# A list-scheduled attention and MLP kernel: the sign step of the weight unpacking gets a place outside the softplus/erf stretches, and the dates of many other steps move

## The chip, the cores and the metric

The kernel runs on one core of a Trainium2 chip. The metric is device time in microseconds (us). The core's engines are TensorE (PE, with its weight loads as PEld), VectorE (DVE), ScalarE (ACT), GpSimd (POOL) and SyncE (SP, which here issues nearly all DMAs). Each engine works through its own instructions in the order in which the program lists them, and waits at each for what that instruction needs.

## The reference

A linear ("random feature") attention over 8 x 8 heads gives x, and a gated MLP follows it. Cut to what matters:

```
phi(x)  = exp(x @ omega.T - |x|^2/2 - max) / sqrt(128)     # 128 features, head width 64
attn    = (phi(q) @ (phi(k).T @ v)) / (phi(q) @ sum(phi(k)) + 1e-6)    # 8 x 8 heads, 576 tokens
x       = attn, laid out as 4608 tokens x 512
h       = x @ w_in                                         # 512 -> 2048
g       = h * erf(softplus(h))
out     = g @ w_out                                        # 2048 -> 512
```

## The kernel before

**Work and tiles.** The heads are taken in 32 pairs. For a pair, `project` makes the features (tiles `ppk`, `ppq`, then `fk`, `fq` by exponentials on ACT), `key_values` sums keys times values (`kvp`, copied to `kh`), `turn` transposes the query features (`pt`, copied to `qh`), and `attend` multiplies both (`nd`) and divides by way of a logarithm and an exponential on ACT (`rc`), which gives `xs`. The 4608 tokens form six groups, `SUPERS`: groups 0 and 1 with half-widths of 288 columns, groups 2 to 5 with 432. In groups 2 to 5 the projections are done with seven instead of eight block products (a scheme with sums of blocks: `hX`, `hY`, `hZ`, and `oX`, `oY`, `oZ` from group 3 on). Groups 0 and 1 use the plain products `h` (names h000 to h110) and `o`. Every product of fp32 numbers is made of three matmuls on a high and a low part (`xh`, `xl`; `gh`, `gl`; the two halves of a weight tile `w`).

**Softplus/erf stretches.** Each group is cut into four quarters of the 2048 hidden units, so there are 24 stretches (`chain`). A stretch is four ACT instructions on the `gs` tiles: softplus, softplus, erf, erf. The two functions are in two different activation tables, and the exponentials and logarithms of the attention are in a third; an `ACT_TABLE_LOAD` stands wherever the table has to change. Then DVE or POOL multiplies (`gate`: `hs<-gs,hs`), and `high`/`rest` split the result into `gh`/`gl`. In groups 3 to 5 (eleven stretches) the steps `gsum` first form differences of blocks in `gs`, and `th`, `tl`, `bh`, `bl`, `bb` are split from them. The tile names carry group and granule: the second stretch of group 0 works on gs0_2 and gs0_3, the third on gs0_4 and gs0_5.

**Weights.** The weights come in as 64-bit words. In group 0 and at the start of group 1, `make` unpacks each of 32 tiles: a DMA (`st`), then `pbias` on ACT, an `ACTIVATE` with the function Prelu that brings in sign and exponent (`wt<-st`), `ptail` (`st<-st`) and `pjoin` (`wt<-wt,st`) on DVE, `phigh` on ACT or DVE (the high half of `w`), `prest` on DVE (the low half), and a store. Only then can TensorE use the tile. Later uses fetch the finished tile back. w1_... are tiles of the first projection and w2_... of the second; w2_0_3_0 and w2_0_3_1 are the last tiles that the first and the second quarter's `o` use.

**What sets the order.** `Plan.order` writes every engine's instruction list before anything runs. Each step has a due time; a list of small shifts (`JITTER`) moves the due times of steps in a window; distances between engines (`LAG`), buffer numbers and the options (which engines a step may go to, at what cost, with how much slack) do the rest. A step may name the activation table it needs (`set`). While a softplus/erf stretch is under way, only steps without a `set` may be placed on ACT, and a change of table is charged `COST["table"]`. Where the plan itself returns to the exponential's table, it writes the load; other loads are added when the program is built, wherever an instruction's function isn't in the table that is loaded. In the kernel before, `pbias` names no table.

All engines' instructions go through one helper, so the line in the rows is the same everywhere (L1015 before, L1049 after); tiles tell them apart.

## Time and profile before

| | before |
|---|---|
| median of 3 runs | 1029.24 us (1028.66 to 1030.05) |
| the profiled execution, its own time | 1027.2 us |
| its span in the trace | 1025.4 us |
| mean granted TensorE clock (1.0 is 2.4 GHz) | 0.997 |
| PE busy | 1003.5 us (98%) |
| PEld / DVE / ACT / POOL busy | 932.8 / 795.0 / 688.5 / 612.9 us |
| activation table loads | 72, together 92.4 us |
| first matmul starts, last one ends | 3.74 us, 1021.13 us |

The span is the profiled execution between its first and last instruction; 1.8 us of the execution's own time lie outside it. Busy times are sums over the whole span, so the share says little on any one place. PE busy counts an instruction until its modelled end, so it doesn't tell fast matmuls from slow ones.

### The profile page before, as it was taken

The page shows a single profiled execution, that of the slowest core. Times are in us where ns is not written, and L with a number is a line of the kernel's source. Part 1 is how long each engine was busy: PE and PEld are TensorE (multiplying, and loading weights), DVE is VectorE, ACT ScalarE, POOL GpSimd, SP SyncE. Part 2 cuts the span into 40 slices and gives each one's busy share as a digit, 9 for nine tenths or more (in the row PEclk, how much of TensorE's full clock was granted, in tenths as well). Part 3 has the DMA queues.
Part 4 walks back from the last instruction along what each step waited for, and adds up shares of the span by engine and source line. Part 5 has one row for each costly group of instructions (what it writes and reads, how often), then busy time and mean ns, then how long its engine had stood idle before and what let it go on. Part 6 is the DMA issues. An engine that isn't in the chain of part 4 may idle for free.

```text
span 1025.4 us, 19428 instructions
## 1 busy us (share of the span) xinstructions
PE 1003.5 (98%) x7132; PEld 932.8 (91%) x7132; DVE 795.0 (78%) x1284; ACT 688.5 (67%) x1295; POOL 612.9 (60%) x446
## 2 busy tenths in 40 slices
PE   8999999999999999999999999999999999999998
PEld 7799889999999999999999888989989999989997
DVE  5788878877876976677787987798887687678664
ACT  8988776787685774765768585677657655644650
POOL 3625443875567816455788356489884668957520
PEclk9999999999999999999999999999999999999999
DMA  8377776699686766676657866656786457686751
GB/s 229 90 267 237 255 239 244 240 320 307 218 298 205 255 213 220 225 243 202 223 187 277 280 224 214 226 199 212 246 278 223 164 185 227 219 288 219 230 180 70
DMA packets 99486, 232.72 MB, mean 227 GB/s; under 512 B 11200, under 2 KB 11712, under 8 KB 99392
## 3 DMA queue, kind: packets, MB, share of 16 engines
q1 hardware_dynamic: 99232, 231.42, 67.5%
q8 instruction: 57, 0.93, 0.4%
q14 instruction: 37, 0.30, 0.1%
q10 hardware_dynamic: 160, 0.07, 0.0%
HBM read 188.45 MB, written 42.99 MB: 226 GB/s over the span
## 4 chain that ended last, share of the span: by engine, by line
PE 84%; DVE 6%; issue 3%; ACT 2%; DMA 2%; POOL 1%; SPq 1%; POOLq 0%; DVEq 0%; ACTq 0%
PE o L1015 17%; PE hX L1015 13%; PE h L1015 10%; PE oX L1015 9%; PE hY L1015 6%; PE nd L1015 5%; PE oY L1015 4%; PE ppq L1015 4%; PE ppk L1015 4%; PE kvp L1015 4%; PE hZ L1015 3%; PE pt L1015 2%; PE oZ L1015 2%; DMA uq<-qT 1%; DVE gs L1015 1%
## 5 line engine op out<-in xcount | busy, mean ns | idle before, releaser
L1015 PE MATMUL o<-gh,w 128*128 128x288 f32 (+1 forms) x832 | 213.5, 329 | 0.6 <-DVE w L1015 0.6
L1015 POOL TENSOR_TENSOR hs<-gs,hs 128x864 f32<-128x864 f32 (+1 forms) x50 | 112.2, 2266 | 106.1 <-ACT gs L1015 85.2
L1015 PE MATMUL hX<-xh,wb 128*128 128x432 f32 x512 | 168.6, 369 | 2.4 <-ACT hs L1015 1.4
L1015 PEld LDWEIGHTS o<-gh,w 128*128 128x128 f32 x832 | 145.2, 188 | 6.4 <-DVE w L1015 1.2
L1015 PE MATMUL o<-gl,w 128*128 128x288 f32 (+1 forms) x416 | 132.9, 319 | 0.1
L1015 PE MATMUL h<-xh,w 128*128 128x288 f32 x512 | 127.9, 318 | 5.0 <-DVE w L1015 4.4
L1015 PEld LDWEIGHTS hX<-xh,wb 128*128 128x128 f32 x512 | 96.2, 188 | 8.6 <-ACT hs L1015 1.8
L1015 POOL TENSOR_TENSOR uq<-uq 128x288 f32<-128x288 f32 (+1 forms) x50 | 50.9, 1038 | 79.2 <-DMA uq<-qN 38.9
L1015 PEld LDWEIGHTS h<-xh,w 128*128 128x128 f32 x512 | 89.0, 193 | 9.5 <-DVE w L1015 5.6
L1015 ACT ACT_TABLE_LOAD x72 | 92.4, 1283 | 2.0 <-PEq L1368 0.7
L1015 PE MATMUL hX<-xl,wb 128*128 128x432 f32 x256 | 91.6, 358 | 0.0
L1015 ACT ACTIVATE fk<-ppk,mxk 128x128 f32<-128x128 f32 x288 | 81.2, 379 | 8.9 <-DVE mxk L1015 8.0
L1015 PE MATMUL hY<-xh,wb 128*128 128x432 f32 x256 | 84.8, 368 | 0.0
L1015 ACT ACTIVATE fq<-ppq,mxq 128x128 f32<-128x128 f32 x288 | 78.1, 386 | 8.2 <-DVE mxq L1015 7.9
L1015 PE MATMUL oX<-th,wb 128*128 128x432 f32 x264 | 82.9, 361 | 0.0
L1015 PEld LDWEIGHTS o<-gl,w 128*128 128x128 f32 x416 | 78.3, 188 | 2.7 <-DVE gl L1015 0.5
L1015 ACT ACTIVATE rc<-nd,eps 64x288 f32<-64x288 f32 x128 | 63.4, 496 | 25.2 <-PE nd L1015 22.2
L1015 ACT ACTIVATE hs<-hX 128x432 f32<-128x432 f32 x71 | 37.1, 529 | 63.2 <-PE hX L1015 62.3
L1015 PE MATMUL nd<-qh,kh 128*128 128x288 f32 x256 | 76.3, 410 | 1.9 <-DVE qh L1015 1.4
L1015 PE MATMUL h<-xl,w 128*128 128x288 f32 x256 | 76.9, 300 | 0.7 <-POOL xl L1015 0.7
L1015 DVE TENSOR_TENSOR xs<-nd,rc 64x288 f32<-64x288 f32 (+1 forms) x160 | 61.2, 393 | 16.6 <-ACT rc L1015 11.1
L1015 ACT ACTIVATE gs<-hs 128x1728 f32<-128x1728 f32 (+1 forms) x48 | 69.4, 1481 | 1.1 <-POOL bl L1015 0.8
(141 smaller groups left out, 2642.4 us busy)
## 6 DMA issues: line engine op xcount, KB each, us to landing
wb<-wdc SPq DMA_DIRECT2D x216, 256.0 KB, 3.6
wb<-wdw SPq DMA_DIRECT2D x162, 256.0 KB, 3.9
w<-wdw SPq DMA_DIRECT2D x52, 512.0 KB, 4.7
st<-w SPq DMA_DIRECT2D x32, 512.0 KB, 4.9
wdw<-w SPq DMA_DIRECT2D x32, 512.0 KB, 4.3
wdc<-c SPq DMA_DIRECT2D x32, 512.0 KB, 4.7
v<-vP SPq DMA_DIRECT2D x32, 325.0 KB, 5.2
uk<-kR SPq DMA_DIRECT2D x24, 320.0 KB, 3.9
```

Of the source, the lines that this page charges most:

```text
L1015: return tc.keep_in_program_order(method(*args, **kwargs))
```

## The change

One step gets a table: `pbias` now says `set="exp"`, so the planner no longer places it inside a softplus/erf stretch. The list of shifts is replaced (15 entries before, five of them empty and the others with the position in the list as their seed; 131 entries now, each with its own seed), and nearly all constants of the planner move a little: the distances `LAG`, the offsets of due times (`DRAIN`, `DIVIDE`, `FIRST`), and the slacks with which a step goes to POOL (`GATES`, `RESTS`, `LATE`, `WHG`) or ACT (`SQA`). What is computed, and each instruction's form, stay; the numbers of some engines' instructions move since steps change engine.

```diff
-LAG = {"T": 0.32725, "A": 0.2525, "V": 0.2605, "G": 0.3105, "S": 0.2904}
+LAG = {"T": 0.33004999999999995, "A": 0.26025, "V": 0.261, "G": 0.3147, "S": 0.32880000000000004}
...
-        for k, (lo, hi, amp) in enumerate(JITTER):
+        for lo, hi, amp, k in JITTER:
...
+JITTER = ((227.5, 727.5, 4, 5), (648.5, 748.5, 1, 874), (712.0, 762.0, 2, 7), (574.9, 594.9, 8, 8),
...
-DRAIN = 2.0
-DIVIDE = 4.0
+DRAIN = 1.83
+DIVIDE = 4.09
...
-GATES = 10.0
-RESTS = 6.0
+GATES = 4.08
+RESTS = 8.91
...
-LATE = 40.0
+LATE = 35.77
...
-SQA = 4.0
-WHG = 5.0
+SQA = 5.62
+WHG = 9.94
...
         pl.op("pbias", [("A", 0.67, -1e9)], lambda e: E.w_bias(e, st, w),
-              reads=[(st, "h")], writes=[(w, 0)])
+              reads=[(st, "h")], writes=[(w, 0)], set="exp")
```

In the two programs' lists the number of `ACT_TABLE_LOAD` goes from 72 to 68. The `gsum` differences go from 20 to 42 instructions on POOL (halves) and from 23 to 12 on DVE, `bl` from 4 to 6 on DVE; TensorE has 5854 matmuls in both.

**The second stretch, on ACT.** Before, from the load ahead of the first softplus to the first erf (gs0_2 and gs0_3 are the stretch's tiles, the rows that write wt... are `pbias`, those that write w... are `phigh`):

```order
L1015 ACT_TABLE_LOAD
L1015 ACTIVATE gs0_2_1296<-hs0_0_2_1036 128x1152
L1015 ACT_TABLE_LOAD
L1015 ACTIVATE wt2_0_3_0_1330<-st2_0_3_0_1218 128x512
L1015 ACTIVATE wt1_1_0_1339<-st1_1_0_1261 128x512
L1015 ACTIVATE kh_1_2_1348<-kvp_1_2_1266 128x2x64
L1015 ACTIVATE kh_1_2_1348<-kvp_1_2_1266 128x128
L1015 ACT_TABLE_LOAD
L1015 ACTIVATE gs0_3_1297<-hs0_0_3_1067 128x1152
L1015 ACTIVATE w2_0_3_0_12_1219<-wt2_0_3_0_1330 128x2x256
L1015 ACT_TABLE_LOAD
L1015 ACTIVATE gs0_2_1296<-gs0_2_1296 128x1152
```

After, from the first softplus's end on; one load stands ahead of these rows, the second is shown, the third follows the erfs:

```order
L1049 ACTIVATE kh_1_2_1304<-kvp_1_2_1265 128x2x64
L1049 ACTIVATE kh_1_2_1304<-kvp_1_2_1265 128x128
L1049 ACTIVATE os0_0_1314<-o0_0_0_0_1225 128x288
L1049 ACTIVATE gs0_3_1263<-hs0_0_3_1068 128x1152
L1049 ACTIVATE os0_0_1314<-o0_0_0_1_1297 128x288
L1049 ACT_TABLE_LOAD
L1049 ACTIVATE gs0_2_1262<-gs0_2_1262 128x1152
L1049 ACTIVATE gs0_3_1263<-gs0_3_1263 128x1152
L1049 ACT_TABLE_LOAD
L1049 ACTIVATE fq_1_2_1389<-ppq_1_2_0_1241,mxq_1_2_1307 128x128 x3
L1049 ACTIVATE fq_1_2_1389<-ppq_1_2_1_1250,mxq_1_2_1307 128x128 x3
L1049 ACTIVATE wt2_0_3_0_1420<-st2_0_3_0_1222 128x512
```

The two `pbias` in the stretch are gone, and with them the load ahead of them and the one behind. wt2_0_3_0 now comes behind six exponentials, and the copies os0_0, which wait for TensorE's `o`, have moved into the stretch.

**The second stretch, on TensorE.** Before, the end of what TensorE has to do until the next weight tiles; w2_0_3 had been used earlier, and w1_1_2 is the next one to come:

```order
L1015 MATMUL h000_1_0_1451<-xh0_1_658,w1_1_0_13_1262 128x288
L1015 MATMUL h000_1_0_1451<-xl0_1_669,w1_1_0_13_1262 128x288
L1015 MATMUL h000_1_0_1451<-xh0_1_658,w1_1_0_13_1262 128x288
L1015 MATMUL ppk_1_3_0_1477<-wqk_70,uk_1_3_1105 128x128 x3
L1015 MATMUL ppk_1_3_1_1485<-wqk_70,uk_1_3_1105 128x128 x3
L1015 MATMUL ppk_1_3_2_1492<-wqk_70,uk_1_3_1105 128x128 x3
L1015 MATMUL pt_1_2_0_1500<-ident_67,fq_1_2_1287 128x128 x3
L1015 MATMUL pt_1_2_1_1516<-ident_67,fq_1_2_1287 128x128 x3
L1015 MATMUL h000_1_1_1523<-xh0_0_526,w1_1_2_15_1386 128x288
```

After, the same transposes stand ahead of the first matmul on w2_0_3, and w1_1_0 comes later still:

```order
L1049 MATMUL o0_0_1_1_1381<-gh0_1_1183,w2_0_1_0_11_1123 128x288
L1049 MATMUL ppk_1_3_0_1403<-wqk_70,uk_1_3_1107 128x128 x3
L1049 MATMUL ppk_1_3_1_1413<-wqk_70,uk_1_3_1107 128x128 x3
L1049 MATMUL ppk_1_3_2_1422<-wqk_70,uk_1_3_1107 128x128 x3
L1049 MATMUL pt_1_2_0_1437<-ident_67,fq_1_2_1389 128x128 x3
L1049 MATMUL o0_0_3_0_1451<-gh0_0_1139,w2_0_3_0_12_1223 128x288
L1049 MATMUL o0_0_3_0_1451<-gl0_0_1160,w2_0_3_0_12_1223 128x288
L1049 MATMUL o0_0_3_0_1451<-gh0_0_1139,w2_0_3_0_12_1223 128x288 x2
L1049 MATMUL o0_0_3_0_1451<-gl0_0_1160,w2_0_3_0_12_1223 128x288
```

The 24 matmuls on w2_0_3 and those on w1_1_0 have moved behind `ppk_1_3` and the first transposes.

**The third stretch.** On ACT, before (gs0_4, gs0_5):

```order
L1015 ACT_TABLE_LOAD
L1015 ACTIVATE gs0_4_1779<-hs0_1_0_1481 128x1152
L1015 ACT_TABLE_LOAD
L1015 ACTIVATE wt2_0_3_1_1811<-st2_0_3_1_1693 128x512
L1015 ACT_TABLE_LOAD
L1015 ACTIVATE gs0_5_1780<-hs0_1_1_1579 128x1152
L1015 ACTIVATE w2_0_3_1_20_1694<-wt2_0_3_1_1811 128x2x256
L1015 ACT_TABLE_LOAD
L1015 ACTIVATE gs0_4_1779<-gs0_4_1779 128x1152
L1015 ACTIVATE gs0_5_1780<-gs0_5_1780 128x1152
L1015 ACTIVATE wt1_1_4_1885<-st1_1_4_1764 128x512
```

After:

```order
L1049 ACT_TABLE_LOAD
L1049 ACTIVATE gs0_4_1783<-hs0_1_0_1553 128x1152
L1049 ACTIVATE gs0_5_1784<-hs0_1_1_1606 128x1152
L1049 ACT_TABLE_LOAD
L1049 ACTIVATE gs0_4_1783<-gs0_4_1783 128x1152
L1049 ACTIVATE gs0_5_1784<-gs0_5_1784 128x1152
L1049 ACT_TABLE_LOAD
L1049 ACTIVATE wt2_0_3_1_1867<-st2_0_3_1_1716 128x512
L1049 ACTIVATE wt1_1_4_1889<-st1_1_4_1772 128x512
L1049 ACTIVATE qh_1_3_1899<-pt_1_3_0_1893 128x384
L1049 ACTIVATE gh0_5_1902<-hs0_1_1_1606 128x1152
L1049 ACTIVATE qh_1_3_1899<-pt_1_3_1_1904 128x384
L1049 ACTIVATE w2_0_3_1_20_1717<-wt2_0_3_1_1867 128x2x256
```

wt2_0_3_1 has moved out of the stretch and stands behind both erfs and a load; its high half (the last row) is now behind two copies `qh` and a split `gh`. On TensorE after, w2_0_3_1 is needed here:

```order
L1049 MATMUL ppk_2_0_2_1876<-wr_71,uk_2_0_1431 128x128
L1049 MATMUL ppk_2_0_1_1887<-wr_71,uk_2_0_1431 128x128
L1049 MATMUL pt_1_3_0_1893<-ident_67,fq_1_3_1671 128x128 x3
L1049 MATMUL pt_1_3_1_1904<-ident_67,fq_1_3_1671 128x128 x3
L1049 MATMUL pt_1_3_2_1919<-ident_67,fq_1_3_1671 128x128 x3
L1049 MATMUL nd_1_3_0_0_1933<-qh_1_3_1899,kh_1_3_1755 128x288
L1049 MATMUL o0_1_3_0_1939<-gh0_2_1442,w2_0_3_1_20_1717 128x288
L1049 MATMUL o0_1_3_0_1939<-gl0_2_1457,w2_0_3_1_20_1717 128x288
L1049 MATMUL o0_1_3_0_1939<-gh0_2_1442,w2_0_3_1_20_1717 128x288 x2
```

Before, the matmuls on that tile stood ahead of `ppk_2_0` and these transposes, and matmuls on w1_1_4 followed the first of them.

**Between the attention phase and the first projection, on TensorE.** Before (pt_0_3 are the last transposes of the phase, `h000_0_0` is the first product of the projection):

```order
L1015 MATMUL pt_0_3_2_605<-ident_67,fq_0_3_550 128x128 x3
L1015 MATMUL nd_0_3_0_0_615<-qh_0_3_609,kh_0_3_564 128x288
L1015 MATMUL nd_0_3_1_0_622<-qh_0_3_609,kh_0_3_564 128x288
L1015 MATMUL nd_0_3_0_1_624<-qh_0_3_609,kh_0_3_564 128x288
L1015 MATMUL nd_0_3_1_1_632<-qh_0_3_609,kh_0_3_564 128x288
L1015 MATMUL h000_0_0_639<-xh0_0_526,w1_0_0_1_143 128x288
L1015 MATMUL h000_0_0_639<-xl0_0_555,w1_0_0_1_143 128x288
L1015 MATMUL h000_0_0_639<-xh0_0_526,w1_0_0_1_143 128x288
L1015 MATMUL ppq_1_0_0_651<-wqk_70,uq_1_0_187 128x128 x3
```

After:

```order
L1049 MATMUL pt_0_3_2_628<-ident_67,fq_0_3_571 128x128 x3
L1049 MATMUL h000_0_0_634<-xh0_0_547,w1_0_0_1_128 128x288
L1049 MATMUL h000_0_0_634<-xl0_0_576,w1_0_0_1_128 128x288
L1049 MATMUL h000_0_0_634<-xh0_0_547,w1_0_0_1_128 128x288
L1049 MATMUL nd_0_3_0_0_642<-qh_0_3_632,kh_0_3_585 128x288
L1049 MATMUL nd_0_3_1_0_649<-qh_0_3_632,kh_0_3_585 128x288
L1049 MATMUL nd_0_3_0_1_651<-qh_0_3_632,kh_0_3_585 128x288
L1049 MATMUL nd_0_3_1_1_656<-qh_0_3_632,kh_0_3_585 128x288
```

The first three matmuls of `h000_0_0` have moved ahead of `nd_0_3`, into the place where `nd_0_3` waits for the copy `qh_0_3`; behind `nd_0_3` now stand nine matmuls (of `h000_0_1`, `h010_0_0` and `h010_0_1`) ahead of `ppq_1_0`, where before there were three, and the first that needs the second half of x (xl0_1) comes after it as before.

## Rows read from the trace of the kernel before

**Rows 1.** Busy time by stretch (window, us, then PE, PEld, DVE, ACT, POOL; clock).

```profile
115.00:118.30 3.30, 3.30 (x14) 3.02 (x13) 3.13 (x5) 1.81 (x4) 3.30 (x4) 0.50 0.99 365
156.00:159.20 3.20, 3.20 (x15) 3.20 (x15) 3.06 (x8) 2.27 (x5) 0.15 (x1) 0.50 0.94 324
700.00:1000.00 300.00, 295.76 (x1659) 277.82 (x1658) 232.30 (x301) 179.61 (x237) 203.47 (x103) 1.00 0.67 221
```

**Rows 2.** Timeline, ACT, second softplus/erf stretch: start, us, instruction.

```profile
98.23 1.19 ACT L1015 ACTIVATE wt<-st 128x512 f32<-128x512 f32 x2
...
99.79 1.28 ACT L1015 ACT_TABLE_LOAD   x1
...
104.05 2.22 ACT L1015 ACTIVATE gs<-gs 128x1152 f32<-128x1152 f32 x2
...
107.58 1.66 ACT L1015 ACTIVATE fq<-ppq,mxq 128x128 f32<-128x128 f32 x6
109.10 1.27 ACT L1015 ACTIVATE wt<-st 128x512 f32<-128x512 f32 x2
```

**Rows 3.** Timeline, TensorE, the same stretch; waits stand in brackets.

```profile
92.99 1.38 PE L1015 MATMUL kvp<-v,fk 128*64 128x130 f32 x36
...
95.06 0.42 PE L1015 MATMUL o<-gh,w 128*128 128x288 f32 x2
...
108.54 2.17 PE L1015 MATMUL ppk<-wqk,uk 128*128 128x128 f32 x18
...
113.55 0.40 PE L1015 MATMUL h<-xh,w 128*128 128x288 f32 x1 [2.18 <-DVE w L1015]
```

**Rows 4.** Timeline, DVE, the same stretch.

```profile
110.57 1.27 DVE L1015 SCALAR_TENSOR_TENSOR wt<-wt,st 128x512 int32<-128x512 int32 x2
...
112.83 0.67 DVE L1015 CAST w<-wt 128x512 fp32r<-128x512 f32 x1
...
115.71 0.54 DVE L1015 TENSOR_REDUCE mxk<-ppk 128x3 f32<-128x384 f32 x1
```

**Rows 5.** Timeline, TensorE, third softplus/erf stretch.

```profile
145.44 1.58 PE L1015 MATMUL ppk<-wr,uk 64*128 64x128 f32 x18
...
148.56 0.40 PE L1015 MATMUL h<-xh,w 128*128 128x288 f32 x1 [0.78 <-DVE w L1015]
...
150.99 0.91 PE L1015 MATMUL pt<-ident,fq 128*128 128x128 f32 x6 [0.56 <-DVE qh L1015]
...
152.99 0.40 PE L1015 MATMUL h<-xh,w 128*128 128x288 f32 x1 [0.60 <-ACT qh L1015]
...
154.80 0.54 PE L1015 MATMUL h<-xh,w 128*128 128x288 f32 x2 [1.28 <-DVE w L1015]
```

**Rows 6.** Timeline, ACT, third stretch.

```profile
147.51 1.16 ACT L1015 ACTIVATE gh<-hs 128x1152 fp32r<-128x1152 f32 x1 [2.44 <-POOL hs L1015]
...
151.57 0.49 ACT L1015 ACTIVATE qh<-pt 128x384 f32<-128x384 f32 x1 [0.43 <-PE pt L1015]
```

**Rows 7.** Timeline, TensorE, the attention phase ahead of the first projection.

```profile
43.90 0.75 PE L1015 MATMUL nd<-qh,kh 128*128 128x288 f32 x2 [1.15 <-DVE qh L1015]
...
50.15 0.41 PE L1015 MATMUL h<-xl,w 128*128 128x288 f32 x1 [0.73 <-POOL xl L1015]
```

**Rows 8.** Groups by line and form: output matmuls of 288 columns, all of the run.

```profile
L1015 PE MATMUL o<-gh,w 128*128 128x288 f32 x512 | 115.9, 305 | 0.6 <-DVE w L1015 0.6
```

**Rows 9.** Timeline, TensorE, the three longest waits after 300 us.

```profile
763.46 0.55 PE L1015 MATMUL pt<-ident,fq 128*128 128x128 f32 x3 [1.85 <-DVE hs L1015]
...
910.39 0.46 PE L1015 MATMUL hX<-xh,wb 128*128 128x432 f32 x1 [1.41 <-ACT hs L1015]
...
974.60 0.46 PE L1015 MATMUL hX<-xh,wb 128*128 128x432 f32 x1 [0.97 <-DVE hs L1015]
```

**Rows 10.** Timeline, DVE, ahead of the first of them.

```profile
759.01 3.87 DVE L1015 TENSOR_TENSOR bl<-hs,bh 128x1728 fp32r<-128x1728 f32 x1
```

**Rows 11.** One tile's instructions on DVE (min, median, max ns).

```profile
L1015 DVE TENSOR_TENSOR bl<-hs,bh x4: 1947/2618/3867, 759.0 to 939.1; 128x1728 fp32r<-128x1728 f32 x4
```

More of the change, by code (lines that the diff above doesn't have):

```diff
@@ L320, in whole_ @@
     return n < WHOLE or WHOLE2[0] <= n < WHOLE2[1]
-JITTER = ((0, 0, 0), (186.1, 206.1, 4), (0, 0, 0), (0, 0, 0), (0, 0, 0), (227.5, 727.5, 4),
-          (648.5, 748.5, 1), (712.0, 762.0, 2), (574.9, 594.9, 8), (27.8, 47.8, 0.5), (390.5, 440.5, 8),
-          (458.1, 558.1, 8), (876.3, 896.3, 2), (0, 0, 0), (616.6, 816.6, 1))
+JITTER = ((227.5, 727.5, 4, 5), (648.5, 748.5, 1, 874), (712.0, 762.0, 2, 7), (574.9, 594.9, 8, 8),
[36 rows of a table added]
 AHEAD = 40.56
 SPANS = ((0, 288), (288, 288))
-DRAIN = 2.0
-DIVIDE = 4.0
+DRAIN = 1.83
+DIVIDE = 4.09
 WHOLE = 32
@@ L336 @@
 PAIR = 8.0
-FIRST = 11.5
+FIRST = 11.32
 LEAD = 30.0
-START0 = 4 * FIRST + 5
-GATES = 10.0
-RESTS = 6.0
+START0 = 51.0
+GATES = 4.08
+RESTS = 8.91
 EARLY = (0, 0)
```

36 rows, old and new, of the table JITTER are left out of this document.

## The prediction

> **What bounds the kernel now.** TensorE is busy 98% of the span (table above), so the first view was the timeline of TensorE, and in it only the rows with a wait in brackets: a microsecond won anywhere else is worth nothing unless it ends one of these. From 160 to 760 us there is hardly any. What remains lies in four places: where the attention phase hands over to the first projection [rows 7], in the second and third softplus/erf stretch of group 0 [rows 3, 5], and in three late stretches of the groups with seven products [rows 9]; one small pair of waits lies near 223 us [rows 8]. Second I read the granted clock by stretch [rows 1]: behind the waits of the second and third stretch it is 0.50 (the lower level, 1.2 GHz) for 3.3 and 3.2 us, and over the late stretches, where TensorE waits for 1.85, 1.41 and 0.97 us [rows 9], it is 1.00. So the two stretches cost more than their waits: half of 3.3 us, 1.65 us, each. Last come the timelines of ACT and DVE for the two stretches [rows 2, 4, 6], to see what is late there: a weight tile, whose `pbias`, join and cast follow one another on ACT and DVE. None of these waits names a DMA, so SP's moved transfers enter no term.
>
> **The two loads in a stretch.** Before, ACT changes its table for softplus, for `pbias`, again for softplus, for erf, and back. Two of the five changes go. A change costs 1.3 us: the two erfs start at 104.05 and last 2.22, and the exponentials behind the load start at 107.58 [rows 2]. That takes 2.6 us off ACT in each of two stretches, 5.2 us in all. It isn't the gain: `pbias` of two tiles leaves the stretch too and comes later, and TensorE's order around it is another.
>
> The Trainium skill (ScalarE: Activation LUTs, What ACT_TABLE_LOAD costs) puts a change at 1.28 us of load and 1.38 us of drain, 2.66 us. The trace doesn't agree: from the end of the erfs to the exponentials only 1.31 us pass [rows 2]. By the page the two changes left behind the copies in the second stretch and the three in the third would end 2.8 and 4.1 us later than I count below, and 1023 would become 1029.9, no change; with the row against it I give that 1 in 100.
>
> **Second stretch after.** I count from the last matmul of h110_0_3. Ahead of w2_0_3 TensorE has 69 matmuls of `o`, nine `ppq`, eighteen `kvp`, nine `ppk` and three `pt` (counted in the program's list). 100 matmuls of 288 columns lie between 95.06 and 108.54 [rows 3], 0.135 us each: 9.3. `ppk` took 2.0 (to the first `pt`: 113.55 less the wait of 2.18 is 111.37, and six `pt` fill the last 0.8), `ppq` is its like, `kvp` 1.3, three `pt` 0.4. Sum 15.0 us. On ACT the copy of os0_0 now stands in the stretch and must wait for the thirteenth `o`, behind `ppq` and `kvp`: 1.75 + 2.0 + 1.3 = 5.05, and 0.2 until it is seen. Then: copy 0.4 (an estimate, from 0.49 for 384 columns [rows 6]), softplus 1.1 (as an erf), copy 0.4, load 1.3, two erfs 2.2, load 1.3, six exponentials 1.65, `pbias` 0.6 [rows 2]: 14.2. On DVE: join 0.65, one reduction `mxk` 0.54, cast 0.67 [rows 4], with 0.1 until DVE sees it: 16.2. TensorE therefore waits 1.2 us, and for the low half, 0.65 later, another 0.4 (two matmuls hide the rest): 1.6 in place of 2.2. Gain 0.6. Bounds: ACT without the hold at the copy would be about 1 us earlier, 0.5 in all; one more reduction and a copy ahead of the join on DVE make it 2.7.
>
> **Third stretch after.** From the last matmul of h110_1_1, TensorE has 69 `o` (9.3), the short `ppk` (1.55 [rows 5]) and three `pt` (0.4): 11.25; the other six `pt` fit under the copy `qh` that `nd` waits for, and `nd` ends near 12.2. ACT: load 1.3, two softplus 2.2, load 1.3, two erfs 2.2, load 1.3, two `pbias` 1.2: 9.6 with 0.1 at the start. Then it stands until the `pt` at 11.4, copies `qh` (0.49), splits `gh` (1.16 [rows 6]), copies `qh` again (0.45), and only then makes the high half of w2_0_3_1 (0.6): 14.1. TensorE waits 1.9, and 0.4 for the low half: 2.3, in place of 0.78 + 0.56 + 0.60 + 1.28 = 3.2 [rows 5]. Gain 0.9, bounds 0.4 (DVE gives the join late) and 1.6 (`gh` overlaps). So what this stretch wins on table loads it partly gives back to the `qh`, `gh`, `qh` in front of the high half; `nd`, `rc` and the next group's features queue behind them on ACT.
>
> **The clock.** It fell behind the waits of the two stretches [rows 1]. The second stretch's new 1.2 us is nearest to the 1.41 us after which it held [rows 1, 9]: I count 1.65 won there. The third's 1.9 and 0.4 lie between 1.85, after which it held, and 2.18, after which it fell [rows 3]; in the present third stretch it fell after several waits of 3.2 together. I take no gain there. Bounds: both kept, 0; both won, 3.3.
>
> **Start.** Three matmuls of `h`, 0.4 us, move into the wait of 1.15 for `qh` [rows 7], and nine instead of three stand ahead of `ppq` and so ahead of the place that waits 0.73 for xl: 0.8 us more cover, the 0.73 goes. Gain 1.1; 0 if the new order waits for w1_0_2, which those nine need, 1.9 if both waits go.
>
> **Near 223 us.** The first stretch of group 1 waits 0.6 in two pieces for a tile [rows 8]. In the new order far more work of TensorE stands ahead of that tile's use. Gain 0.6; 0 at worst.
>
> **Late stretches.** The rest moves: differences `gsum` from DVE to POOL, two more `bl` to DVE, copies between ACT and DVE. In the two orders none of the three causes stands where it stood: the `bl` of 3.87 us [rows 10], ahead of which 763.46 waits, is on POOL after. But eleven stretches get a new order, and three in eleven waited before: 4.2 us. I take two such waits of the middle size, 1.41, that is 2.8, gain 1.4; bounds none (gain 4.2) and twice as many (loss 4.2).
>
> **Sum.** 1.1 + 0.6 + 1.65 + 0.9 + 0.6 + 1.4 = 6.25 us. The profiled execution, 1027.2 by its own time, would take 1021.0. It lies 2 us under the median of its runs, 1029.24, which becomes 1023.0. With all bounds good the gain is 1.9 + 1.7 + 3.3 + 1.6 + 0.6 + 4.2 = 13.3, time 1016; with all bad it is 0 - 0.5 + 0 + 0.4 + 0 - 4.2, time 1033.5.
>
> **Rivals.** *The weights stay the limit* (chance 0.12): `pbias` comes later by as much as the loads save, both waits and both falls of the clock stay, and only 1.7 us at the start and at 223 remain: 1027.5. For it: in the third stretch 2.6 us off ACT turn into 0.9. Against it: in the second the count has a margin of 1 us.
>
> *Slower* (0.12): DVE and POOL in the late stretches. The same `bl` instruction takes 1.95 to 3.87 us [rows 11], and the longest of them is the one that held TensorE. The new order puts six `bl` and, in the first stretch of group 5, all four `gsum` on DVE, and has POOL at 22 more `gsum` halves beside it. With the late waits unchanged I have 1024.4; five further waits of 1.41 in the eleven stretches, eight instead of three, bring 1031.4. From there on it is slower; against it, `gsum` as a whole leaves DVE.
>
> The Trainium skill (GPSIMD Engine Reference, Specifications) says that POOL shares its SBUF interfaces with VectorE, with contention for DVE instructions with two SBUF inputs, as `bl` and `gsum` are. The spread of `bl` [rows 11] agrees with it; no row here separates it from other causes.
>
> *More* (0.18): no late wait and no fall of the clock in the third stretch: 1023.0 - 2.8 - 1.65 = 1018.5.
>
> **Numbers.** That leaves 0.57 for the forecast, with its own range of 1020 to 1026. A measurement here tells about 0.2% (2.1 us) from nothing, so the forecast and *more* are faster, the weights' rival is the same (0.13 with the page's rule), *slower* is slower. Range 1017 to 1030: it leaves out the slower case and the lower part of *more*.
>
> **What would show it.** Four loads fewer, 68. TensorE's wait ahead of the first `o` on w2_0_3 about 1.2 us at some 15 us behind h110_0_3, and the clock at 1.00 there; in the third stretch a wait for ACT's `w` of nearly 2 us and again 3 us at 0.50; ACT idle before the copies os0_0. Wrong if waits after 700 us sum to more than 7 us, or if one of the two stretches waits over 3 us.

## The result, and the profile after

| | before | after |
|---|---|---|
| median of the runs shown with the result (4 each) | 1028.95 us (1027.81 to 1030.05) | 1017.67 us (1017.22 to 1021.53) |
| the profiled execution, its own time | 1027.2 us | 1017.87 us |
| its span | 1025.4 us | 1016.1 us |
| last matmul ends | 1021.13 us | 1011.78 us |
| mean granted clock | 0.997 | 1.000 |
| table loads | 72 | 68, together 87.2 us |

The changed kernel is faster by about 1%: ratio 0.9906, 95% interval 0.9889 to 0.9923. The medians lie 11.3 us apart, the two profiled executions 9.3 us.

As with the kernel before, TensorE's timeline is read first, for its waits (in brackets, with what ended them). Apart from the one ahead of the first matmul, these are all waits of 0.4 us or more in the profile of the changed kernel:

```profile
6.52 2.93 PE L1049 MATMUL ppk<-wqk,uk 128*128 128x128 f32 x12 [1.00 <-ACT uk L1049]
46.59 0.72 PE L1049 MATMUL nd<-qh,kh 128*128 128x288 f32 x2 [1.26 <-DVE qh L1049]
108.75 0.37 PE L1049 MATMUL o<-gh,w 128*128 128x288 f32 x1 [1.72 <-ACT gh L1049]
117.81 0.53 PE L1049 MATMUL h<-xh,w 128*128 128x288 f32 x2 [0.82 <-DVE w L1049]
146.30 0.40 PE L1049 MATMUL o<-gh,w 128*128 128x288 f32 x1 [1.16 <-ACT w L1049]
147.51 0.54 PE L1049 MATMUL o<-gh,w 128*128 128x288 f32 x2 [0.68 <-DVE w L1049]
152.85 0.41 PE L1049 MATMUL h<-xh,w 128*128 128x288 f32 x1 [2.19 <-ACT fk L1049]
717.02 0.55 PE L1049 MATMUL pt<-ident,fq 128*128 128x128 f32 x3 [0.45 <-DVE hs L1049]
```

The reader is to see three things. The waits of the two stretches are not gone, they have moved: 1.72 us ahead of w2_0_3 where 2.18 stood ahead of w1_1_2 [rows 3], and 1.16, 0.68 and 2.19 us in the third stretch where 0.78, 0.56, 0.60 and 1.28 stood [rows 5]. The wait of 0.73 us for xl [rows 7] and those near 223 us [rows 8] are gone. And between 153 us and the end there is one wait of 0.4 us or more, of 0.45 us, where before had three of 1.85, 1.41 and 0.97 [rows 9].

The view by stretch gives window and length, busy time of PE (and its matmuls), granted clock, share of the DMA engines, GB/s. Behind the waits of both stretches the clock is 1.00 in this execution, where it was 0.50 [rows 1]:

```profile
112.00:116.00 4.00, 4.00 (x28) 3.74 (x27) 3.60 (x8) 3.08 (x10) 4.00 (x5) 1.00 0.99 390
...
152.00:156.00 4.00, 3.15 (x22) 3.04 (x23) 3.62 (x8) 3.74 (x13) 0.00 (x0) 1.00 0.77 274
```

**The second stretch** is late by one DVE instruction. In DVE's timeline two reductions `mxk` stand ahead of the join of w2_0_3_0 (its `pbias` on ACT starts at 105.55 and lasts 0.70), and a third stands between the join and the cast. I had counted one reduction in all. The cast ends at 108.60, and the `o` starts at 108.75; the row of TensorE names ACT's gh, but that one (gh0_0) was ready earlier: the `o` on w2_0_0 have used it.

```profile
105.93 1.01 DVE L1049 TENSOR_REDUCE mxk<-ppk 128x3 f32<-128x384 f32 x2
106.86 0.68 DVE L1049 SCALAR_TENSOR_TENSOR wt<-wt,st 128x512 int32<-128x512 int32 x1
107.46 0.54 DVE L1049 TENSOR_REDUCE mxk<-ppk 128x3 f32<-128x384 f32 x1
107.92 0.68 DVE L1049 CAST w<-wt 128x512 fp32r<-128x512 f32 x1
```

**The third stretch** goes on ACT as counted, `qh`, `gh`, `qh`, then the high half of w2_0_3_1, and then something comes that I hadn't counted:

```profile
139.72 1.28 ACT L1049 ACT_TABLE_LOAD   x1
141.02 1.18 ACT L1049 ACTIVATE wt<-st 128x512 f32<-128x512 f32 x2
143.83 0.49 ACT L1049 ACTIVATE qh<-pt 128x384 f32<-128x384 f32 x1 [1.64 <-PE pt L1049]
144.22 1.16 ACT L1049 ACTIVATE gh<-hs 128x1152 fp32r<-128x1152 f32 x1
...
145.64 1.09 ACT L1049 ACTIVATE w<-wt 128x512 fp32r<-128x512 f32 x2
...
150.99 0.65 ACT L1049 ACTIVATE wt<-st 128x512 f32<-128x512 f32 x1 [1.94 <-DMA st<-w]
151.66 2.43 ACT L1049 ACTIVATE fk<-ppk,mxk 128x128 f32<-128x128 f32 x9
```

The `pbias` of a later tile, w1_1_6, waits 1.94 us for its DMA. The exponentials `fk` queue behind it on ACT; they hold the PSUM tile `ppk`, and TensorE's next `h` waits 2.19 us for that.

**Where the 9.3 us came from.** I put the matmuls of both kernels in program order and compared the times at which equal amounts of matmul work were done (each matmul counted at the median distance to the next, over both traces, of its kind). Up to the end of the first stretch the changed kernel is 1.0 us later: it loses 2.1 in the first 30 us, nearly all of it in the first 13, and recovers 0.7 where the attention hands over to the first projection and 0.4 near 91 us. Then it wins 1.3 us in the second stretch, 1.3 in the third, 1.8 between 173 and 240 us (near 223), some 0.7 from there to 750 us, and 5.1 in the late stretches: 9.2 in all, and its last matmul ends 9.35 us earlier. Since the orders differ, each of these is good to about half a microsecond. They also compare one execution with one: the pieces at the start and in the two stretches differ between executions of one and the same order by up to 3.2 us (e3 to e5 below), those near 223 us and in the late stretches by half a microsecond or less.

### The profile page after: what moved, and what is told of

Read it like the earlier page. It is cut to its first block, busy times and chain, and to the rows that moved or that the text cites. A ratio compares the mean times of both kernels' runs of the same rounds, so it can differ in the third digit from the quotient of the medians.

```text
span 1016.1 us, 19442 instructions
## 1 busy us (share of the span) xinstructions
PE 997.5 (98%) x7132; PEld 929.5 (91%) x7132; DVE 787.5 (78%) x1287; ACT 685.9 (68%) x1290; POOL 611.7 (60%) x460
## 4 chain that ended last, share of the span: by engine, by line
PE 93%; DVE 2%; ACT 2%; POOL 1%; DMA 1%; issue 1%; SPq 0%; ACTq 0%; DVEq 0%
PE o L1049 17%; PE hX L1049 15%; PE oX L1049 10%; PE h L1049 10%; PE hY L1049 7%; PE nd L1049 6%; PE oY L1049 5%; PE ppq L1049 5%; PE ppk L1049 4%; PE kvp L1049 4%; PE hZ L1049 4%; PE oZ L1049 3%; PE pt L1049 3%; ACT gs L1049 1%; DMA st<-w 1%
## 5 line engine op out<-in xcount | busy, mean ns | idle before, releaser
L1049 PE MATMUL o<-gh,w 128*128 128x288 f32 (+1 forms) x832 | 217.9, 330 | 3.7 <-ACT gh L1049 1.7
L1049 PE MATMUL hX<-xh,wb 128*128 128x432 f32 x512 | 170.7, 368 | 0.0
L1049 POOL TENSOR_TENSOR hs<-gs,hs 128x864 f32<-128x864 f32 (+1 forms) x50 | 104.6, 2114 | 99.0 <-ACT gs L1049 93.6
L1049 PE MATMUL h<-xh,w 128*128 128x288 f32 x512 | 123.9, 312 | 3.0 <-ACT fk L1049 2.2
L1049 POOL TENSOR_TENSOR uq<-uq 128x288 f32<-128x288 f32 (+1 forms) x50 | 56.4, 1146 | 66.8 <-DMA uq<-qN 40.8
L1049 PEld LDWEIGHTS h<-xh,w 128*128 128x128 f32 x512 | 86.7, 188 | 6.3 <-ACT fk L1049 2.4
L1049 ACT ACT_TABLE_LOAD x68 | 87.2, 1283 | 2.5 <-PEq L1402 0.7
L1049 PE MATMUL oX<-th,wb 128*128 128x432 f32 x264 | 88.7, 368 | 0.1
L1049 PE MATMUL hY<-xh,wb 128*128 128x432 f32 x256 | 87.4, 369 | 0.0
L1049 POOL TENSOR_TENSOR uk<-uk 128x288 f32<-128x288 f32 (+1 forms) x54 | 51.5, 973 | 38.3 <-DMA uk<-kT 18.8
```

What stands on the lines that cost most here:

```text
L1049: return tc.keep_in_program_order(method(*args, **kwargs))
```

## The experiments

Two kinds were run: single steps moved by hand in a list that otherwise stays, and parts of the change taken alone or left out, for which the planner writes a new list. For all of them the table gives, from the profiled execution, TensorE's waits of 0.3 us or more before and after 200 us (the one ahead of the first matmul left out), and the mean clock. The ratio is to the kernel before on the same chip.

| kernel | waits to 200 us | waits after 200 us (longest) | clock | median, us | ratio, 95% interval |
|---|---|---|---|---|---|
| before | 7.3 | 4.6 (1.85) | 0.997 | 1028.95 | 1 |
| after | 8.8 | 0.45 (0.45) | 1.000 | 1017.67 | 0.9906 [0.9889, 0.9923] |
| e1_set_only | 11.1 | 10.2 (2.38) | 0.994 | 1032.72 | 1.0065 [1.0042, 1.0087] |
| e2_all_but_set | 5.5 | 9.6 (2.73) | 0.996 | 1030.47 | 1.0025 [1.0006, 1.0043] |
| e3_stretch2_by_hand | 11.0 | 4.5 (1.85) | 0.997 | 1028.13 | 1.0003 [0.9989, 1.0016] |
| e4_late_waits_mended | 9.6 | 1.3 (0.95) | 0.998 | 1024.46 | 0.9968 [0.9954, 0.9982] |
| e5_after_again | 6.5 | 0.46 (0.46) | 0.998 | 1017.32 | 0.9895 [0.9879, 0.9911] |
| e6_start_mended | 7.2 | 0.45 (0.45) | 0.998 | 1016.03 | 0.9892 [0.9873, 0.9911] |
| e7_exp_ahead | 7.7 | 0.39 (0.39) | 0.996 | 1019.0 | 0.9912 [0.9898, 0.9926] |
| e8_all_mended | 6.4 | 0.44 (0.44) | 0.997 | 1017.42 | 0.9895 [0.9878, 0.9911] |
| e9_less_mid | 7.3 | 9.2 (2.74) | 0.996 | 1034.0 | 1.0072 [1.006, 1.0085] |
| e10_less_late | 7.7 | 2.35 (1.91) | 0.998 | 1020.81 | 0.9943 [0.9931, 0.9956] |
| e11_old_list | 9.9 | 13.8 (3.11) | 0.989 | 1045.66 | 1.0194 [1.0177, 1.0212] |
| e12_new_list | 7.8 | 12.6 (2.71) | 0.998 | 1036.89 | 1.0105 [1.009, 1.0121] |

The kernel before had a median of 1026.72 us beside e1 to e4, 1028.58 beside e5 to e8 and 1026.35 beside e9 to e12.

### The two parts of the change alone (e1, e2)

The first is the kernel before with the table on the sign step and nothing else; the second is the changed kernel without it.

```diff
 e1_set_only, against before:
-              reads=[(st, "h")], writes=[(w, 0)])
+              reads=[(st, "h")], writes=[(w, 0)], set="exp")
 e2_all_but_set, against after:
-              reads=[(st, "h")], writes=[(w, 0)], set="exp")
+              reads=[(st, "h")], writes=[(w, 0)])
```

> The kernel before with the one edit set="exp" on pbias; list of shifts and all constants as before, order planned anew. Theory A (the 11 us come from the late stretches, about 4 us of waits, from the two falls of the clock, 3.3 us, and from many small pieces; what leaves the softplus/erf stretch comes back as weights that are late): 68 to 70 loads, but no more than 4 us faster than before, 1025 to 1031, with waits for w or behind it in the stretches of group 0 still over 3 us together. Theory L (the table loads inside the stretches are what cost): 1017 to 1022.

> The changed kernel without set="exp"; new shifts and constants, order planned anew, so pbias may stand in a stretch again. A: within 4 us of the changed kernel, 1015 to 1022, with the late stretches free of long waits unless the new order upsets them. L: 1024 or more.

Neither part alone is faster than before: 1.0065 with the set, 1.0025 with the list and the constants. Neither theory survives. A wanted 1015 to 1022 us for e2, which took 1030.5; its range for e1, 1025 to 1031, is missed too, by 1.7 us. L wanted 1017 to 1022 for e1, which has the 68 loads and is slower than before; that e2, with 70 loads, takes more than 1024 fits L, but not by way of the loads. In both, new waits stand late in the run, far from the stretches. Two rows of e1's timeline of TensorE:

```profile
574.76 0.46 PE L1015 MATMUL hX<-xh,wb 128*128 128x432 f32 x1 [1.86 <-DVE hs L1015]
...
985.16 0.46 PE L1015 MATMUL hX<-xh,wb 128*128 128x432 f32 x1 [2.38 <-DVE hs L1015]
```

and two of e2's:

```profile
710.25 0.46 PE L1049 MATMUL hZ<-xh,wb 128*128 128x432 f32 x1 [1.60 <-ACT fq L1049]
...
883.35 0.60 PE L1049 MATMUL hX<-xh,wb 128*128 128x432 f32 x1 [2.73 <-DVE hs L1049]
```

### The set's work by hand in the old order (e3)

Everything stays where it was before, but the two sign steps leave the second stretch: that of w2_0_3_0 goes ahead of the first softplus, that of w1_1_0 behind the second erf, and the join, high and rest of w1_1_0 follow on DVE behind a copy os0_1. Two loads fall away (70).

```diff
+MOVES = [(('pbias', 'wt2_0_3_0'), 'ahead', ('sp', 'gs0_2')),
+         (('prest', 'wt1_1_0'), 'behind', ('oout', 'o0_0_1_1')),
...
+         (('pbias', 'wt1_1_0'), 'behind', ('erf!', 'gs0_3'))]
...
-    for o in plan.order(slots, CAPS):
+    for o in moved(plan.order(slots, CAPS)):
```

> The kernel before, its order kept but for five moves in the second stretch: pbias of w2_0_3_0 ahead of the first softplus, pbias of w1_1_0 behind the second erf, its join, high and rest behind one copy on DVE. 70 loads, nothing else moved. L: ACT is 2.6 us ahead behind the stretch, so TensorE's wait of 2.18 us at 113 us goes and the clock holds there: 3.9 us faster, 1025.1. A rival, that DVE's join and cast set the date whatever ACT does: the wait stays over 1 us, and the time is within 1.5 us of before.

No change, and the wait is still there: 2.38 us, with the clock at 0.57 from 117 to 121 us. ACT gave up two loads, and the date did not move with it. TensorE waits for the high half of w1_1_2 here, as before. ACT is done with the two `pbias` of the tiles concerned at 110.75, 3.2 us ahead of their joins; before, the joins followed 0.2 us behind [rows 2, 4]. DVE's timeline shows why it comes no earlier; the joins of w1_1_1 and w1_1_2 (two in one row) start only at 113.90, behind a `ptail` of 1.57 us and copies that fill DVE without a gap, and the cast of w1_1_2 is the last row:

```profile
112.05 1.57 DVE L1032 TENSOR_SCALAR st<-st 128x512 int32<-128x512 int32 x1
113.53 0.44 DVE L1032 COPY hs<-h 128x288 f32<-128x288 f32 x1
113.90 1.28 DVE L1032 SCALAR_TENSOR_TENSOR wt<-wt,st 128x512 int32<-128x512 int32 x2
115.09 0.67 DVE L1032 CAST w<-wt 128x512 fp32r<-128x512 f32 x1
115.69 0.54 DVE L1032 COPY qh<-pt 128x384 f32<-128x384 f32 x1
116.16 0.67 DVE L1032 CAST w<-wt 128x512 fp32r<-128x512 f32 x1
```

So 2.6 us off ACT in a stretch won nothing here. It is not the price of the loads alone: the join, high and rest of w1_1_0, which came later with its sign step, take DVE from 107.66 to 109.80, at the head of the work that fills it up to the cast. A version in which they stay out of the way was not run.

Compared at equal work, e3's profile lies 3.2 us behind before's at 30 us, ahead of any moved step, and 3.1 behind at the end; e4's lies 2.7 behind at 30 us. The order up to there is the same in all three. The execution of before that was profiled had a short start, which is part of why the medians lie further apart than the profiled executions.

### The late waits alone (e4)

In the order of before, three steps move by a place or a few: the `bl` of 3.87 us [rows 10] goes behind the sum of hZ that TensorE waited for, a `th` goes behind two copies hX, and a copy hX ahead of a `bb`.

```diff
+MOVES = [(('rest', 'bl4_0'), 'behind', ('hadd', 'hZ4_0_3')),
+         (('high', 'th5_0_0'), 'behind', ('hout', 'hX5_0_3', 1)),
+         (('hout', 'hX5_1_3', 0), 'ahead', ('rest', 'bb5_2'))]
```

> The kernel before, its order kept but for three moves: bl4_0 on DVE behind the sum hZ4_0_3, th5_0_0 on ACT behind two copies hX, and a copy hX5_1_3 on DVE ahead of bb5_2. A: the waits of 1.85, 1.41 and 0.97 us go and nothing takes their place: 4.2 us faster, 1024.8. Rival: bl, th and bb are late in turn and TensorE waits for them in oX and oZ instead: within 1.5 us of before.

The waits of 1.41 and 0.97 us are gone, and of the 1.85 there is 0.95 left (the row below, TensorE's timeline). The waits removed sum to 3.3 us (0.90 + 1.41 + 0.97). Compared at equal work, e4's profile is 1.2 us behind before's at 750 us and 2.1 ahead at the end: 3.3 us won there, so a late wait costs its length. The time falls by 0.32% of 1026.72, also 3.3 us, but with an interval of 1.8 to 4.7; the medians lie 2.3 apart.

```profile
765.31 0.47 PE L1030 MATMUL hX<-xh,wb 128*128 128x432 f32 x1 [0.95 <-DVE hs L1030]
```

This profile shows one more thing, on the clock. TensorE's wait in the second stretch is that of before, 2.19 us where [rows 3] have 2.18, and this time the clock held (the row of the timeline, then the view by stretch, PE alone):

```profile
116.23 0.41 PE L1030 MATMUL h<-xh,w 128*128 128x288 f32 x1 [2.19 <-DVE w L1030]
...
116.00:122.00 6.00, 5.59 (x37) 1.00 0.80 296
```

### The changed kernel mended by hand (e5 to e8)

e5 is the changed kernel itself once more. In e6 the third part of the first keys is loaded and squared ahead of the queries, on SP and ACT; in e7 the sign step of w1_1_6, which waits for its DMA, goes behind most of the exponentials `fk` (eight of nine in the trace); e8 has both, and moves of the copies in the second stretch and of w2_0_3_1's join, high and low part in the third.

```diff
 e6_start_mended:
+MOVES = [(('loadk', 'uk_0_0', 2), 'ahead', ('loadq', 'uq_0_0', 0)),
+         (('sqk', 'uk_0_0', 2), 'ahead', ('sqq', 'uq_0_0', 0))]
 e7_exp_ahead:
+MOVES = [(('expk', 'ppk_2_0_0'), 'ahead', ('pbias', 'wt1_1_6')),
+         (('expk', 'ppk_2_0_2'), 'ahead', ('pbias', 'wt1_1_6'))]
 e8_all_mended: both, and
+         (('sp', 'gs0_3'), 'ahead', ('kvhigh', 'kh_1_2')),
+         (('oout', 'o0_0_0_1'), 'behind', ('erf', 'gs0_2')),
+         (('pjoin', 'wt2_0_3_1'), 'ahead', ('high', 'gh0_4')),
+         (('phigh', 'wt2_0_3_1'), 'ahead', ('high', 'gh0_5')),
...
```

> The changed kernel itself, as the measure for the next three on the same chip: 0.990 of before, some 1016.5 where before takes 1026.7.

> The changed kernel's order with two moves: SP loads the third part of uk_0_0 ahead of uq_0_0, and ACT squares it ahead of uq_0_0, as in the kernel before. If the wait of 1.00 us at 5.51 us is what lets the first 13 us end 2 us later than before: 1 to 2 us faster than the changed kernel. If the start is bound by DMA and ACT as a whole: no difference over 0.5 us.

> The changed kernel's order with one instruction moved on ACT: pbias of w1_1_6, which stands 1.94 us for its DMA, goes behind six of the nine exponentials fk_2_0. If the wait of 2.19 us of TensorE at 150.67 us is a PSUM bank that those exponentials free: 1.5 to 2.1 us faster than the changed kernel. If it is the weight or DMA in truth: the wait moves to w1_1_6 and the time stays within 0.5 us.

> The changed kernel's order with both of these and two more: in the second stretch softplus of gs0_3 goes ahead of the copies kh and os, and the second copy os0_0 between the erfs; in the third, w2_0_3_1 gets its join, high and low part ahead of gh0_4 and gh0_5. If the waits counted in the prediction are caused as it says (1.72 us by the hold of ACT at the copies, 1.16 and 0.68 us by the splits ahead of the weight): 5 to 6 us faster than the changed kernel, 1010 to 1012. If DVE or DMA stand behind them: 2 us or less.

e6 ends the wait of 1.00 us in the first 13 us: TensorE's first row is now one run of 18 matmuls.

```profile
3.81 4.40 PE L1063 MATMUL ppk<-wqk,uk 128*128 128x128 f32 x18 [3.81 <-ACT uk L1063]
```

Its median is 1.3 us under that of e5, three of its five runs (1015.84 to 1016.03) are below all of e5's (1016.96 to 1017.77) and two (1017.97, 1018.31) above: it is the fastest version seen, but the two times can't be told apart for certain. The start itself can: the first `kvp` begins at 10.26 us in e6 and at 10.39 in e8, which has the same two moves, and at 11.54 to 12.81 in five executions without them (after, e5, e7, e9, e10).

e5's clock by stretch (PE alone) contradicts a part of my reading of the result. Behind a wait of 1.72 us, the same as in the first profile, the clock fell this time:

```profile
108.00:112.00 4.00, 3.77 (x20) 0.74 0.99 375
112.00:116.00 4.00, 4.00 (x26) 0.83 0.98 336
```

The time did not suffer, 1017.77 for this execution: compared at equal work, e5 loses 1.4 us to the first profile in the second stretch and wins 1.4 in the third, where the wait of 2.19 us is one of 0.26 (a further one of 0.29 names a weight tile). The `pbias` of w1_1_6 didn't wait for its DMA this time. In e6 it did, for less long than in the first profile; one row of ACT and one of TensorE from e6, then TensorE's from e5:

```profile
149.19 0.65 ACT L1063 ACTIVATE wt<-st 128x512 f32<-128x512 f32 x1 [0.94 <-DMA st<-w]
151.06 0.40 PE L1063 MATMUL h<-xh,w 128*128 128x288 f32 x1 [1.22 <-ACT fk L1063]
...
151.67 0.40 PE L1049 MATMUL h<-xh,w 128*128 128x288 f32 x1 [0.26 <-ACT fk L1049]
```

Waits for the DMA of 1.94, 0.94 and none go with waits of TensorE of 2.19, 1.22 and 0.26 us, and the `h` starts 1.2 us behind the first `fk` each time: that is the chain from the DMA by way of ACT to TensorE. e9 (below) has the same order up to here and the long wait for the DMA, yet a short one of TensorE, because there the clock fell in the third stretch and TensorE came later itself. ACT, TensorE, and the clock by stretch (PE alone):

```profile
150.72 0.65 ACT L1049 ACTIVATE wt<-st 128x512 f32<-128x512 f32 x1 [1.86 <-DMA st<-w]
152.58 0.40 PE L1049 MATMUL h<-xh,w 128*128 128x288 f32 x1 [0.67 <-ACT fk L1049]
...
148.00:152.00 4.00, 3.91 (x19) 0.57 0.90 358
```

So a fall of the clock and a wait behind it don't add up here: the fall takes 1.7 us of TensorE's work (4 us at 0.57), and the wait is shorter by 1.5.

e7 takes the `fk` out from behind that `pbias`, and is 1.7 us slower than e5, which neither of its two theories has. In e5, with which it is compared, TensorE's wait for the `fk` was only 0.26 us, so there was little to win, and the chain above isn't put to the test. The low half of w2_0_3_1 comes 0.89 instead of 0.67 us late, another 0.57 follows, and the clock falls in the third stretch as well:

```profile
148.00:152.00 4.00, 3.60 (x19) 3.60 (x20) 3.28 (x8) 3.39 (x10) 3.24 (x3) 0.71 0.92 333
152.00:156.00 4.00, 3.43 (x20) 2.87 (x19) 2.90 (x6) 2.79 (x7) 0.00 (x0) 0.86 0.60 229
```

All five of its executions are slower than all of e5's, those with a mean clock of 0.998 too; why stays open.

e8 has the same time as e5. Its waits in the second and third stretch are 1.40, 0.64, 1.17, 0.68 and 1.18 us, and its clock fell twice (0.79 from 104 to 112 us, 0.60 from 152 to 156).

Two of e8's moves did not do what they were meant to. The second softplus stayed behind the copies of kh and os0_0 on ACT: the first softplus of a stretch lists both `gs` tiles among its own, so the move found that one, which stood ahead already. And in the third stretch TensorE's 1.17 us now ends with ACT's copy qh and not with the weight. So the time is as its second theory has it, 2 us or less, but what the first one asked isn't settled. In these four the early waits (6.4 to 7.7 us up to 200 us) were not won by moving single steps: the next wait stands close behind.

### One shift, and the list and the constants apart (e9 to e12)

After e1 and e2 a new theory was needed: the list of 131 shifts and the constants have been picked together for one order in which nothing waits late, and any edit of the planner's input gives another order. e9 and e10 take out one shift each, e11 and e12 cross the list and the constants.

```diff
 e9_less_mid, against after:
-          (-1.2, 48.8, 4, 684), (261.1, 361.1, 2, 621), (306.3, 326.3, 4, 633), (309.9, 509.9, 0.5, 966),
+          (-1.2, 48.8, 4, 684), (306.3, 326.3, 4, 633), (309.9, 509.9, 0.5, 966),
 e10_less_late, against after:
-          (944.3, 994.3, 2, 802), (372.5, 422.5, 1, 41), (417.8, 437.8, 1, 641), (276.9, 286.9, 2, 637),
+          (372.5, 422.5, 1, 41), (417.8, 437.8, 1, 641), (276.9, 286.9, 2, 637),
 e11_old_list: after, with the 15 shifts of before
 e12_new_list: after, with LAG, DRAIN, DIVIDE, FIRST, START0, GATES, RESTS, LATE, SQA, WHG of before
```

> The changed kernel with one of its 131 shifts taken out, (261.1, 361.1, 2, 621). The order of all five engines stays as it was until about 235 us (the o of the second group on its third quarter's tiles), and from there on nearly everything stands elsewhere. Theory 'fitted order' (the gain is that of one order out of many, chosen because nothing waits in it after 223 us): the first 230 us as in the changed kernel, but waits of TensorE after 240 us that sum to 2 to 7 us, and a time of 1019 to 1026 us, ratio 0.991 to 0.997. Rival 'rule' (the table kept out of the stretches and the new distances and slacks carry the gain, and one shift more or less is nothing): under 1 us of waits after 240 us, 1016.5 to 1018.5 us.

> The changed kernel without the shift (944.3, 994.3, 2, 802). Only the order of the last 65 us or so moves. Theory 'fitted order': a wait of 0.5 to 2.5 us after 945 us, 1018 to 1020 us. Rival 'rule': no wait after 945 us, 1017 to 1018 us. The spread between the two is close to what runs of one kernel differ by, so the waits decide and the time is only beside them.

> The set of the sign step and all new constants (distances, offsets, slacks), with the old list of 15 shifts. 68 loads. Theory 'fitted order': the constants alone are another draw, 1022 to 1036 us, ratio 0.994 to 1.008, with waits strewn over the run that sum to over 8 us after the first 60 us. Rival 'rule': the constants and the set carry most of the gain, 1017 to 1021 us.

> The set of the sign step and the new list of 131 shifts, with all the old constants. 68 loads. Theory 'fitted order': the list without the constants for which it was picked is another draw, 1022 to 1036 us, ratio 0.994 to 1.008. Rival 'list': the list itself carries the gain, 1017 to 1021 us.

The rivals fall in all four. The theory has the direction each time and too small a size: 1034.0, 1020.8, 1045.7 and 1036.9 us all lie above its ranges. e9 shares the order of the changed kernel up to 235 us, where it is 0.3 us ahead at equal work, and it ends 14.7 us later (last matmul 1026.44 against 1011.78), worse than the 2 to 9 us that I expected. Its waits after 200 us sum to 9.2 us; behind the longest the clock falls too (0.83 from 880 to 890 us, 1.7 us); the remaining 4 us or so lie in shorter gaps and somewhat longer matmul distances that I didn't resolve. The longest wait, in TensorE's timeline:

```profile
885.82 0.73 PE L1049 MATMUL hX<-xh,wb 128*128 128x432 f32 x1 [2.74 <-DVE hs L1049]
```

and what stands ahead of it on DVE, where the sums `hs<-hZ` and `hs<-hX` free the PSUM tile that TensorE wants:

```profile
876.69 2.87 DVE L1049 TENSOR_TENSOR gs<-hs,gs 128x864 f32<-128x864 f32 x1 [2.11 <-POOL gs L1049]
879.49 2.92 DVE L1049 TENSOR_TENSOR bb<-hs,bb 128x864 fp32r<-128x864 f32 x1
882.33 0.60 DVE L1049 TENSOR_TENSOR hs<-hZ,hs 128x432 f32<-128x432 f32 x1
882.85 2.40 DVE L1049 TENSOR_TENSOR gs<-hs,hs 128x864 f32<-128x864 f32 x1
885.17 0.59 DVE L1049 TENSOR_TENSOR hs<-hX,hs 128x432 f32<-128x432 f32 x1
```

The two sums take 0.6 us each. They come late because DVE first waits 2.11 us for a difference that POOL writes, and then does long steps that none of TensorE's waits here names. It is the pattern of the `bl` of before [rows 9, 10]: a short step that frees a bank, behind a long one, in an order that is fixed beforehand. e10 moves only the last 65 us and gets a wait of another kind, 1.91 us for a low half `gl` that DVE finishes late:

```profile
995.80 0.47 PE L1049 MATMUL o<-gl,w 128*128 128x432 f32 x1 [1.91 <-DVE gl L1049]
```

In e10's profile the last matmul ends 3.0 us later than in e5's, 1.9 of it this wait; 0.8 stood already at 980 us. e11 is the slowest of all, with waits of other kinds, for a weight's DMA and for an exponential that is late on ACT:

```profile
348.16 0.37 PE L1015 MATMUL o<-gh,w 128*128 128x288 f32 x1 [2.97 <-DMA w<-wdw]
...
367.86 2.43 PE L1015 MATMUL kvp<-v,fk 128*64 128x130 f32 x36 [3.11 <-ACT fq L1015]
```

## Why the prediction was right, and where its terms were off

The sign was right, and the time of the profiled execution came out at 1017.87 where the sum gave 1021.0. What came was not the likeliest case but the rival *more*: no late wait to speak of, and in the profiled execution no fall of the clock in the third stretch. The gain is 11.3 us where 6.25 were forecast, and the median lies 0.7 us inside the range's lower end. That it came out so near is in part luck: the start was 2.1 us worse than its term and the late stretches 3.7 better, and the clock, worth 1.65 in the sum, fell or held from execution to execution. The median is 5.3 us under the forecast of 1023.0: 3.1 of these are the terms below, and 2.2 the step from the profiled execution to the median. I added the 2 us by which the profile of before lay under its median; after, the profile lies 0.2 us above.

| term | forecast, us | measured, us | the same with e5's profile for after's |
|---|---|---|---|
| start and handover | +1.1 | -1.0 | -0.4 |
| second stretch: waits and clock | +0.6, +1.65 | +1.35 together | -0.1 together |
| third stretch: waits and clock | +0.9, 0 | +1.3 together | +2.6 together |
| near 223 us | +0.6 | +1.8 | +1.4 |
| 240 to 750 us | none | +0.7 | +0.4 |
| late stretches | +1.4 | +5.1 | +5.4 |

- **The loads.** Right: 68, and their 5.2 us are not the gain. e1 has all four fewer and is slower than before; e3 has two fewer in the second stretch, ratio 1.0003, though work on DVE moved with the sign step there. The Trainium skill (ScalarE: Activation LUTs, What ACT_TABLE_LOAD costs) has 2.66 us for a change; after as before the trace doesn't agree, with a load at 139.72 between erfs that end at 139.71 and a `pbias` that starts at 141.02.
- **The start.** The handover brought 0.7 of its 1.1, and only by one of its two parts: the 0.73 for xl is gone, but the wait for `qh`, into which three matmuls moved, is 1.26 us where it was 1.15. Another 0.4 near 91 us isn't in the term. What I didn't look at was the first step of all: the third part of the first keys now comes behind the queries on SP and ACT, and TensorE waits 1.00 us for it and runs its first steps more slowly. e6 removes it. I had sought the start's price only where before waited, and by the sentence that SP's moved transfers enter no term I had left out just this.
- **The second stretch.** A wait of 1.2 and 0.4 was forecast, 1.72 and 0.13 came: the bound that I named, one more reduction ahead of the join on DVE. A wait that I didn't name, 0.82 us for the next weight tile of `h`, took the rest: together 2.67 us of waits, more than the 2.18 of before. What was won here is the clock alone, in the first profile and not in e5, behind the same 1.72 us. The prediction told from the length of a wait whether the clock falls; that step fails, since it fell behind 2.18 us in before and held behind 2.19 in e4.
- **The third stretch.** 2.3 forecast, 1.16 + 0.68 = 1.84 measured, by the mechanism forecast. The step that failed is again the sentence that no wait names a DMA and so SP's moved transfers enter no term: a `pbias` that stands in the queue ahead of the exponentials makes ACT wait 1.94 us for a DMA, and TensorE 2.19. The clock, which I took as kept low there, was 1.00, as in e5 and e6; in e7, e9 and e10 it fell.
- **Late stretches.** The mis-sized term. "I take two such waits of the middle size" had no row behind it; it is the step in which an order that I couldn't time was given the waits of the old one. e4 shows what the three old waits are worth (3.3 us with 0.95 of the 4.2 left), and the changed kernel has none of them. Whether moving `gsum` to POOL has a part in that was not run by itself. The waits after 200 us fall from 4.6 to 0.45; the other microsecond of the 5.1 lies in shorter gaps.
- **The rival *slower*** was closer than its 0.12 says. Five orders from the same planner that nobody had picked by their late waits (e1, e2, e9, e11, e12) have 9.2 to 13.8 us of them, and all five are slower than before, by 0.25 to 1.9%. Its cause, DVE in the late stretches, is what e9's rows show for the longest wait, though not by `bl`: the sums that free PSUM come late behind differences and splits.

So the gain is that of this one order. It is shown that the set alone doesn't carry it (e1), nor any two of set, list and constants (e2, e11, e12), and that the order without one shift in 131 has lost more than the whole gain (e9). The list alone and the constants alone were not run. How such an order was found isn't seen in any trace; that it must have been searched for is argued from the five others. Open stays why the clock falls behind a wait of 1.72 us in one execution and not in another, the part of e9's loss that isn't in waits of 0.3 us or more, and why e7 is slower.

## What to carry to other kernels

When a planner writes the order of a program, a change to its input is a change of the whole program: read the new order's waits over the full run, not the place that the edit names, and take one shift out as a control before giving the gain to a rule. To learn what one step is worth, freeze the list and move that step by hand; e4's three moves paid what the removed waits had cost, while every re-planned version came out slower than the kernel that it edits: e1 by 0.65% against before, the others against the changed kernel by about 0.4% (e10), 1.2 (e2), 1.7 (e9), 2.0 (e12) and 2.9 (e11), from the ratios in the table. Short steps that free a PSUM bank belong ahead of long ones that nobody waits for: in before, e1, e2, e9, e11 and e12 the longest wait after 500 us names a sum or copy `hs` on DVE.

## What the hardware showed

- The granted clock behind the same wait differs from run to run. Behind 1.71 to 1.72 us in the second stretch of one order it was 1.00 from 104 to 116 us in the first profile, in e9 and in e10, and fell in e5 (0.74 and 0.83 in the 4 us slices from 108 to 116), e6 (0.66 from 108 to 112) and e7 (0.59 from 108 to 112). Behind 2.18 us it fell in before, behind 2.19 it held in e4. A term of 1.65 us should carry a chance, not a yes or no.
- One and the same order has different waits where a DMA is in the chain: the `pbias` of w1_1_6 waited 1.94 us for its DMA in one execution of the changed kernel, 0.94 in e6 and not at all in e5, and the `h` behind `fk` waited 2.19, 1.22 and 0.26 us.
- A fall of the clock and a later wait offset each other: in e9 and e10 the `pbias` waited 1.86 and 1.73 us, but the clock was 0.57 and 0.58 from 148 to 152 us and the `h` waited only 0.67 and 0.34. The execution with the clock at 1.000 and the wait of 2.19 us took 1017.87 us, that with a fallen clock in the second stretch and 0.26 us took 1017.77.
